# Two-layer spectral MLP on one core: background work kept out of a block's last two steps, activations and table work tied behind other instructions

## The chip, the cores and the metric

The kernel runs on one core of a Trainium2 chip. The metric is the device time of one launch in microseconds (us). Three runs of the kernel before gave 1007.89, 1008.41 and 1009.72 us, so the median is 1008.41 us. One more execution was recorded by the profiler; every row below is from that one.

## The reference, cut to what matters

```python
X = np.fft.fft(x, axis=1); X = np.fft.fft(X, axis=2)   # x: 2 x 3008 x 256
x = X.real.reshape(6016, 256)
h = x @ w_in;  x = np.maximum(h, 0.0) ** 2 @ w_out      # first layer, d_ff 2048
h = x @ w_in2; out = (h - np.tanh(h)) @ w_out2          # second layer, d_ff 2048
```

## The kernel before, in words

Every matrix product is made of three products of split numbers: an operand is held as a high part (an fp32r copy) and a low part (the operand minus that copy). Work on the 6016 positions goes in 8 blocks of twice 376 or 378 columns. The first 508 us of the trace hold the transform and the first layer, the rest the second layer.

The first layer is a list of 128 steps, `STEPS`: step i is a pair (block, f), f being one of 16 slices of the hidden dimension. The order is block 0 (f 0 to 3) in steps 0 to 3, block 1 in steps 4 to 19, the rest of block 0 in steps 20 to 31, and then blocks 2 to 7 with 16 steps each. So a block, or a part of block 0, ends in steps 3, 19, 31, 47, 63, 79, 95, 111 and 127. Steps 20, 48 and 80 begin with the transform of the next two blocks (lines L352 writing `a`), which keeps TensorE busy for 7 to 10 us.

Step i of the loop runs these parts:

- `front` of step i+2 on TensorE (L352, 6 matmuls into `w`);
- for the steps in `MADE` one slice of `w_in` is made: `transform_in` (L247) needs the bits that `conv` assembled on VectorE (L227, L229, L231);
- `mid` of step i+2: three sums on VectorE (L490, L491, L492, each with an operand in PSUM), then on ScalarE a Relu (L498) and two squares (L499 writes the high part `gh`, L500 the full square);
- `back` of step i on TensorE (L520): 8 matmuls with `gh` of step i and 4 with `gl` of step i-1, and in a block's last step 4 more with its own `gl`. The first step of a block needs the accumulators `a` free;
- after a block's last step `evac`: ScalarE copies two accumulators and VectorE the other two (L551) to `y`, and a DMA stores them;
- `late` of step i+1: the low part `gl` on GpSimd (L509, 1.925 us on average), in the first steps on VectorE.

Beside that runs background work that later stages need. It is cut into pieces by Python generators, and each step takes one or two pieces: `bg0` (rows of the transform's even half, `xf`, L319 to L328), `bg1` (the next batch, L302 to L328), `bg2` (L337), `bg3` (the second layer's weights: the bits in L227 to L231, the low parts in L578, sums of quarters in L586 to L595), and `x7_next` (the second layer's input of a block, L616 to L638). Nearly all of it runs on VectorE, with one operand copy on ScalarE (L219, L335, L576, L593, L623) that feeds it or waits for it.

The order on each engine is not the order of the program: a scheduler lists the instructions by its own estimate, and may put a later instruction in front. `tc.issue_after(ins)` is the one rein: the instructions traced in its block stand behind `ins` on the engine of `ins`. The loop already used it with the last sum of the step's `mid` (`last_mid`, on VectorE) for the pieces of `bg0` to `bg3`, except where a step needs all the rest at once (steps 20, 48 and 80), and not for `x7_next`.

Of the kernel before, what the change touches and what calls it, by code (L numbers as in the profile page):

```python
# [20 lines left out]
NF = DFF // 128  # L21
# [30 lines left out]
STEPS = [(0, f) for f in range(HALF)] + [(1, f) for f in range(NF)]  # L52
# [86 lines left out]
def spectral_mlps(  # L139
# [8 lines left out]
    pe, act, dve, pool, sp = nc.tensor, nc.scalar, nc.vector, nc.gpsimd, nc.sync  # L148
# [36 lines left out]
    def step(gen, k=1000):  # L185
        for _ in range(k):
            if next(gen, "end") == "end":
                return
# [13 lines left out]
    def wt_alloc(layer, f):  # L202
        wt[f] = main.tile([128, 4, 256], F32R, tag=f"wt{f}", name=f"wt{layer}_{f}")
# [246 lines left out]
    last_mid = [None]  # L450
# [60 lines left out]
    def ends(blk, f):  # L511
        return f == NF - 1 or blk == 0 and f in LAST
# [32 lines left out]
    def evac(blk, add=False):  # L545
        n = NC[BLOCKS[blk][1]]
        for m in range(2):
            y = main.tile([128, 2, NM], F32, tag="y", name="y", bufs=2)
            for s in range(2):
                a = acc[1, blk][m][s][:, :n]  # L550
                act.copy(y[:, s, :n], a) if m == 0 else dve.tensor_copy(y[:, s, :n], a)  # L551
            dst = x2_d[blk][:, m, :].rearrange("p (s n) -> p s n", s=2)
            if add:
                pool.dma_start(dst, y[:, :, :n], accum_op=ALU.add)
            else:
                sp.dma_start(dst, y[:, :, :n])

# [231 lines left out]
    n = NC[BLOCKS[0][1]]  # L791
# [10 lines left out]
    def even_rows():  # L802
        for t in range(3):
            yield from folds[t]
            yield from split_even(0, t)

    def next_batch():
        for t in range(3):
            load_x(1, t)
        for t in range(3):  # L810
            yield from fold(1, t)

    def next_even():
        for t in range(3):
            yield from split_even(1, t)

    bg0, bg1, bg2, bg3 = even_rows(), next_batch(), next_even(), make_w2()
# [5 lines left out]
    def look(i):  # L823
        if i < NS and i not in fronts:
            fronts.add(i)
            front(*STEPS[i])

    for i in range(-2, NS - 2):
        blk, f = STEPS[i] if i >= 0 else (0, i)
        if i == max(MADE) + 2:  # L830
            wstack.close()
            pools["w"] = wstack.enter_context(tc.tile_pool(name="psb", bufs=2, space=PSUM))
        look(i + 2)
        if i in MADE:
            p = wps[STEPS[i + 2]]
            w = MADE[i]
            wt_alloc(1, w)
            transform_in(w, p)
            split_transformed_hi(w, p)

        if (blk, f) in DFT:
            for b2 in DFT[blk, f]:
                if b2 == 4:
                    step(bg1)
                    for t in range(3):
                        dft_pair(4, t)
                    step(pair_evac(4))
                else:
                    step(bg0 if b2 < 4 else bg2)
                    dft_mm(b2)  # L850
                    dft_evac(b2)
            look(i + 3)
        mids = mid(*STEPS[i + 2])
        step(mids, 1)
        if i >= 0:
            back(blk, f)
        if i >= 0 and ends(blk, f):
            evac(blk, blk == 0 and f == NF - 1)
        step(mids)
        if i >= -1:  # L860
            late(*STEPS[i + 1])

        if i + 4 in MADE and i + 4 > 1:
            load_raw(1, MADE[i + 4])
        if i in MADE:
            split_transformed_lo(w, p)
            split_hi(w, 2, val[1, w][:, 256:])
        if i + 2 in MADE and i + 2 > -1:
            conv_abs(1, MADE[i + 2])
        if i in MADE:  # L870
            split_lo(w, 2, val[1, w][:, 256:])
            middle_load(w)
        if i == -2:
            middle_add(1)
        if i - 1 in MADE:
            middle_add(MADE[i - 1])
        if i + 1 in MADE and i + 1 > -2:
            step(conv(1, MADE[i + 1]))

        if i >= 8:  # L880
            with tc.issue_after(last_mid[0].ins):
                if i < NF + HALF:
                    step(bg0, 1)
                elif i < 3 * NF:
                    step(bg1, 2)
                else:
                    if blk == 3:
                        step(bg2, 1)
                    step(bg3, 2)
        if blk == NBLK - 1:  # L890
            if f > 0:
                restore(f - 1)
            if f >= 8:
                load_sums(f - 8)
            if f == 3:
                x7_next = make_x7(0)
            if f > 3:
                step(x7_next, 2)

        if i in TABS:  # L900
            for t in range(3):
                load_table(TABS[i], t)
# [21 lines left out]
    for blk in range(NBLK):  # L924
        for j in range(NF // 2):
            if blk < NBLK - 1 and j == 1:
                x7_next = make_x7(blk + 1)
# [31 lines left out]
```

## Time and profile before

| what | value |
|---|---|
| three runs | 1007.89, 1008.41, 1009.72 us |
| the profiled execution's own time | 1006.97 us |
| its span, first to last instruction | 1005.1 us |
| TensorE busy | 963.3 us (96%) |
| VectorE busy | 787.4 us (78%) |
| ScalarE busy | 726.7 us (72%) |
| GpSimd busy | 251.6 us (25%) |
| mean granted TensorE clock | 0.995 |

TensorE is busy nearly all the time, so what can be won is its idle time. It is read by stage, with the engine that each idle time waited for, and then in the timeline around that point.

### The profile page before, as it was taken

The page shows a single profiled execution, that of the slowest core. Times are in us where ns is not written, and L with a number is a line of the kernel's source. Part 1 is how long each engine was busy: PE and PEld are TensorE (multiplying, and loading weights), DVE is VectorE, ACT ScalarE, POOL GpSimd, SP SyncE. Part 2 cuts the span into 40 slices and gives each one's busy share as a digit, 9 for nine tenths or more (in the row PEclk, how much of TensorE's full clock was granted, in tenths as well). Part 3 has the DMA queues.
Part 4 walks back from the last instruction along what each step waited for, and adds up shares of the span by engine and source line. Part 5 has one row for each costly group of instructions (what it writes and reads, how often), then busy time and mean ns, then how long its engine had stood idle before and what let it go on. Part 6 is the DMA issues. An engine that isn't in the chain of part 4 may idle for free.

```text
span 1005.1 us, 15446 instructions
## 1 busy us (share of the span) xinstructions
PE 963.3 (96%) x5542; PEld 950.5 (95%) x5542; DVE 787.4 (78%) x1483; ACT 726.7 (72%) x1289; POOL 251.6 (25%) x171
## 2 busy tenths in 40 slices
PE   4998899899999999999999999999999999999998
PEld 3888898899999999999999999999999999999998
DVE  6999679757988688997576978769787797877766
ACT  2886767787888778897866767667676676766665
POOL 1144614653566546565500000000000000000000
PEclk9999999999999999999999999999999999999999
DMA  8674240205332422417620100001000010000000
GB/s 308 212 228 126 53 142 25 32 1 217 130 130 106 145 85 109 175 73 274 207 94 1 62 1 30 34 1 62 1 32 31 1 63 1 3 29 1 32 1 31
DMA packets 36332, 82.66 MB, mean 82 GB/s; under 512 B 7328, under 2 KB 21152, under 8 KB 36256
## 3 DMA queue, kind: packets, MB, share of 16 engines
q1 hardware_dynamic: 35280, 79.34, 22.5%
q0 software_dynamic: 976, 2.34, 1.4%
q8 instruction: 43, 0.70, 0.3%
q14 instruction: 33, 0.27, 0.1%
HBM read 55.97 MB, written 25.69 MB: 81 GB/s over the span
## 4 chain that ended last, share of the span: by engine, by line
PE 80%; DVE 12%; issue 3%; ACT 2%; DMA 2%; POOL 0%; SPq 0%; DVEq 0%; POOLq 0%; ACTq 0%
PE w L352 32%; PE a L352 29%; PE a L520 18%; DVE pb L490 2%; DVE h L491 2%; DVE h L492 1%; DMA p<-x 1%; DVE val L231 1%; DVE val L229 1%; DMA stage<-w 1%; ACT gh L499 1%; DVE p L321 1%; DVE wt L238 1%; PE w L247 1%; DMA mcol<-wt 0%
## 5 line engine op out<-in xcount | busy, mean ns | idle before, releaser
L509 POOL TENSOR_TENSOR gl<-h,gh 128x752 fp32r<-128x752 f32 (+1 forms) x120 | 230.0, 1925 | 195.2 <-ACT h L500 135.3
L352 PE MATMUL a<-gh,wt 128*128 128x376 f32 (+1 forms) x1024 | 259.7, 335 | 0.0
L520 PE MATMUL a<-gh,wt 128*128 128x376 f32 (+1 forms) x1024 | 204.4, 341 | 15.1 <-ACT gh L499 5.8
L520 PEld LDWEIGHTS a<-gh,wt 128*128 128x128 f32 x1024 | 179.4, 191 | 21.0 <-ACT gh L499 8.7
L352 PEld LDWEIGHTS a<-gh,wt 128*128 128x128 f32 x1024 | 184.7, 188 | 0.0
L352 PE MATMUL a<-gl,wt 128*128 128x376 f32 (+1 forms) x512 | 171.7, 335 | 0.0
L352 PE MATMUL w<-x,sums 128*128 128x376 f32 (+1 forms) x768 | 163.5, 334 | 0.0
L352 PE MATMUL w<-uv,wt 128*128 128x376 f32 (+1 forms) x777 | 157.1, 337 | 1.7 <-POOL wt L259 1.0
L498 ACT ACTIVATE h<-h 128x752 f32<-128x752 f32 (+1 forms) x125 | 103.8, 831 | 59.8 <-DVE h L492 59.1
L673 DVE TENSOR_TENSOR gl<-h,gh 128x376 fp32r<-128x376 f32 (+1 forms) x256 | 138.2, 545 | 11.2 <-ACT gh L671 10.6
L671 ACT CAST gh<-h 128x376 fp32r<-128x376 f32 (+1 forms) x256 | 129.3, 507 | 18.5 <-DVE h L669 17.6
L667 ACT ACTIVATE tanh<-h 128x376 f32<-128x376 f32 (+1 forms) x192 | 99.3, 519 | 56.6 <-DVE h L663 51.9
L352 PEld LDWEIGHTS w<-uv,wt 128*128 128x128 f32 x777 | 136.8, 190 | 2.8 <-POOL wt L259 1.3
L669 DVE TENSOR_TENSOR h<-h,tanh 128x376 f32<-128x376 f32 (+1 forms) x192 | 106.4, 555 | 40.0 <-ACT tanh L667 34.7
L352 PEld LDWEIGHTS w<-x,sums 128*128 128x128 f32 x768 | 135.5, 188 | 0.2 <-ACT u L701 0.2
L490 DVE SCALAR_TENSOR_TENSOR pb<-ub,w,w 128x376 f32<-128x376 f32 (+1 forms) x125 | 75.1, 601 | 56.5 <-PE w L352 48.6
L520 PE MATMUL a<-gl,wt 128*128 128x376 f32 (+1 forms) x512 | 109.1, 336 | 0.5 <-POOL gl L509 0.5
L500 ACT ACTIVATE h<-h 128x752 f32<-128x752 f32 (+1 forms) x128 | 106.8, 834 | 3.0
L499 ACT ACTIVATE gh<-h 128x752 fp32r<-128x752 f32 (+1 forms) x128 | 106.9, 835 | 2.9
L663 DVE TENSOR_TENSOR h<-u,w 128x376 f32<-128x376 f32 (+1 forms) x128 | 69.4, 542 | 38.8 <-ACT u L701 38.8
L352 PEld LDWEIGHTS a<-gl,wt 128*128 128x128 f32 x512 | 96.4, 188 | 0.4 <-DVE gl L673 0.3
L520 PEld LDWEIGHTS a<-gl,wt 128*128 128x128 f32 x512 | 90.8, 190 | 0.8 <-POOL gl L509 0.8
(98 smaller groups left out, 1082.6 us busy)
## 6 DMA issues: line engine op xcount, KB each, us to landing
stage<-w SPq DMA_DIRECT2D x32, 512.0 KB, 3.7
tab<-tab SPq DMA_DIRECT2D x12, 752.0 KB, 7.2
w2s<-w SPq DMA_DIRECT2D x16, 512.0 KB, 2.6
wt<-w2s SPq DMA_DIRECT2D x16, 512.0 KB, 3.6
sums<-sums SPq DMA_DIRECT2D x15, 512.0 KB, 3.8
tab<-tab SPq DMA_DIRECT2D x6, 756.0 KB, 5.4
x<-y SPq DMA_DIRECT2D x12, 376.0 KB, 3.6
x2f<-x SPq DMA_DIRECT2D x6, 752.0 KB, 4.7
```

The source lines that it names most:

```text
L352: pe.matmul(dst, a, r, start=(first and i == 0), stop=(last and i == 3 * len(terms) - 1), **kw)
L490: dve.scalar_tensor_tensor(pb[:, :n], ub[:, :n], w128[:, f:f + 1], bank(p, 0)[:, :n], ALU.mult, ALU.add)
L498: act.activation(h[:, :, :n], h[:, :, :n], AF.Relu)
L499: act.activation(gh[:, :, :n], h[:, :, :n], AF.Square)
L500: act.activation(h[:, :, :n], h[:, :, :n], AF.Square)
L509: eng.tensor_tensor(gl[:, :, :n], h[:, :, :n], f32(gh[:, :, :n]), ALU.subtract)
L520: pe.matmul(acc[1, blk][m][s][:, :n], wt[f][:, wi, m * 128:(m + 1) * 128], g[:, s, :n], start=first and k == 0, stop=last and k == len(par ...
L663: dve.tensor_tensor(h, c, d, ALU.add)
L667: act.activation(th, c, AF.Tanh)
L669: dve.tensor_tensor(h, c, th, ALU.subtract)
L671: act.copy(gh, h)
L673: dve.tensor_tensor(gl, h, f32(gh), ALU.subtract)
```

## The change

The change has four parts. Steps 8 to 17 take two pieces of `bg0` instead of one. No piece of `bg0` to `bg3` runs in a step that ends a block or in the step before (steps 18, 19, 30, 31, 46, 47, 62, 63, 78, 79, 94, 95, 110, 111). The activations of `mid` that are traced in a block's last step stand behind ScalarE's last copy of the accumulators. And the remaining pieces in steps 20 and 80, and those of `x7_next`, stand behind the step's sums.

```diff
@@ evac
-                act.copy(y[:, s, :n], a) if m == 0 else dve.tensor_copy(y[:, s, :n], a)
+                if m == 0:
+                    copied = act.copy(y[:, s, :n], a)
+                else:
+                    dve.tensor_copy(y[:, s, :n], a)
...
+        return copied
@@ the loop over steps
-                    step(bg0 if b2 < 4 else bg2)
+                    with tc.issue_after(last_mid[0].ins):
+                        step(bg0 if b2 < 4 else bg2)
...
-            evac(blk, blk == 0 and f == NF - 1)
+            copied = evac(blk, blk == 0 and f == NF - 1)
+            with tc.issue_after(copied.ins):
+                step(mids)
         step(mids)
...
-        if i >= 8:
+        if i >= 8 and not any(ends(*STEPS[k]) for k in (i, i + 1)):
             with tc.issue_after(last_mid[0].ins):
                 if i < NF + HALF:
-                    step(bg0, 1)
+                    step(bg0, 2)
...
             if f > 3:
-                step(x7_next, 2)
+                with tc.issue_after(last_mid[0].ins):
+                    step(x7_next, 2)
```

VectorE at the end of block 3 (steps 62 to 64), the kernel before. `w` are the sums' operands in PSUM, `w_2926` and `sums` the second layer's weights, `a_2451` and `a_2452` two accumulators.

```order
L578 TENSOR_TENSOR w_2926<-val,w_2926 128x2x256
L586 TENSOR_TENSOR sums<-val 128x128
L587 TENSOR_TENSOR sums<-val 128x128
L490 SCALAR_TENSOR_TENSOR pb<-ub,w_69,w_2964 128x376
L491 TENSOR_TENSOR h<-w_2965,pb 128x376
L492 TENSOR_TENSOR h<-pb,w_2965 128x376
L589 TENSOR_TENSOR sums<-sums,val 128x128
L591 TENSOR_TENSOR sums<-val,sums 128x128
L551 COPY y<-a_2451 128x376
L551 COPY y<-a_2452 128x376
L490 SCALAR_TENSOR_TENSOR pb<-ub,w_69,w_3011 128x376
```

The same place with the change. L554, L582, L590 and L591 are the lines L551, L578, L586 and L587 of before.

```order
L490 SCALAR_TENSOR_TENSOR pb<-ub,w_69,w_2959 128x376
L491 TENSOR_TENSOR h<-w_2960,pb 128x376
L492 TENSOR_TENSOR h<-pb,w_2960 128x376
L554 COPY y<-a_2451 128x376
L554 COPY y<-a_2452 128x376
L490 SCALAR_TENSOR_TENSOR pb<-ub,w_69,w_3002 128x376
L491 TENSOR_TENSOR h<-w_3003,pb 128x376
L492 TENSOR_TENSOR h<-pb,w_3003 128x376
L582 TENSOR_TENSOR w_2926<-val,w_2926 128x2x256
L590 TENSOR_TENSOR sums<-val 128x128
L591 TENSOR_TENSOR sums<-val 128x128
```

Five background instructions left the two steps ahead of the copies; the first three stand in the new block's first step now.

ScalarE at the same end, before: L219 and L593 are background work, the two L551 the copies.

```order
L498 ACTIVATE h<-h 128x2x376
L499 ACTIVATE gh<-h 128x2x376
L219 ACTIVATE val<-stage 128x512
L500 ACTIVATE h<-h 128x2x376
L498 ACTIVATE h<-h 128x2x376
L593 CAST sums<-sums 128x512
L551 COPY y<-a_2449 128x376
L551 COPY y<-a_2450 128x376
L499 ACTIVATE gh<-h 128x2x376
L500 ACTIVATE h<-h 128x2x376
```

And with the change, where L552 is the copy:

```order
L498 ACTIVATE h<-h 128x2x376
L499 ACTIVATE gh<-h 128x2x376
L500 ACTIVATE h<-h 128x2x376
L552 COPY y<-a_2449 128x376
L552 COPY y<-a_2450 128x376
L498 ACTIVATE h<-h 128x2x376
L499 ACTIVATE gh<-h 128x2x376
L500 ACTIVATE h<-h 128x2x376
```

A Relu and a cast that stood ahead of the copies stand behind them or later.

VectorE in steps 9 and 10, before. `xf_835` and its `p` are a fold of the transform, L227 to L231 assemble the bits of a slice of `w_in`.

```order
L490 SCALAR_TENSOR_TENSOR pb<-ub,w_69,w 128x376
L238 TENSOR_TENSOR wt_12_883<-val,wt_12_883 128x256
L491 TENSOR_TENSOR h<-w,pb 128x376
L492 TENSOR_TENSOR h<-pb,w 128x376
L321 TENSOR_TENSOR p<-p 128x256
L227 TENSOR_SCALAR cy<-stage 128x512
L229 SCALAR_TENSOR_TENSOR val<-val,cy 128x512
L231 SCALAR_TENSOR_TENSOR val<-stage,val 128x512
L490 SCALAR_TENSOR_TENSOR pb<-ub,w_69,w 128x376
```

The same stretch with the change:

```order
L492 TENSOR_TENSOR h<-pb,w 128x376
L323 TENSOR_TENSOR xf_835<-p 128x256
L324 TENSOR_TENSOR xf_835<-p 128x1
L326 TENSOR_TENSOR xf_835<-p 128x128
L327 TENSOR_TENSOR xf_835<-p 128x127
L328 TENSOR_TENSOR xf_835<-p 128x1
L238 TENSOR_TENSOR wt_12_888<-val,wt_12_888 128x256
L227 TENSOR_SCALAR cy<-stage 128x512
L229 SCALAR_TENSOR_TENSOR val<-val,cy 128x512
L490 SCALAR_TENSOR_TENSOR pb<-ub,w_69,w 128x376
L231 SCALAR_TENSOR_TENSOR val<-stage,val 128x512
```

Five instructions of the fold come one and two steps earlier, and L231, on which the next L247 of TensorE waits, moves behind the next step's first sum.

## Rows read from the trace of the kernel before

**Rows 1.** Stages: busy us of PE, PEld, DVE, ACT, POOL; clock, DMA share, GB/s.
```profile
56.00:126.00 70.00, 60.55 (x347) 58.37 (x347) 59.72 (x107) 50.12 (x75) 38.18 (x39) 0.95 0.44 125
...
454.00:508.00 54.00, 52.06 (x292) 51.61 (x292) 34.68 (x59) 42.58 (x57) 28.51 (x16) 0.97 0.67 232
508.00:1005.00 497.00, 493.58 (x2859) 492.87 (x2858) 381.72 (x763) 339.18 (x737) 0.00 (x0) 1.00 0.07 24
```
**Rows 2.** Who waited for whom: total us, times, longest us.
```profile
PE w L247 <- DVE val L231: 7.7, 5, 4.0
...
PE a L520 <- ACT gh L499: 5.8, 6, 1.5
...
PE a L520 <- ACT y L551: 5.0, 3, 2.9
...
PE a L520 <- DVE y L551: 4.2, 3, 2.0
```
**Rows 3.** TensorE's timeline: start, duration, line, count, idle before and its releaser.
```profile
178.48 1.68 PE L520 MATMUL a<-gh,wt 128*128 128x378 f32 x8 [2.88 <-ACT y L551]
...
291.05 1.67 PE L520 MATMUL a<-gh,wt 128*128 128x376 f32 x8 [1.75 <-ACT y L551]
...
452.61 1.18 PE L352 MATMUL w<-uv,wt 128*128 128x376 f32 x6
...
455.94 2.04 PE L520 MATMUL a<-gh,wt 128*128 128x376 f32 x7 [1.97 <-DVE y L551]
457.77 2.08 PE L352 MATMUL w<-uv,wt 128*128 128x376 f32 x6
```
**Rows 4.** VectorE's timeline at the end of block 6.
```profile
449.93 1.92 DVE L578 TENSOR_TENSOR w<-val,w 128x512 fp32r<-128x512 f32 x1
...
454.46 0.96 DVE L589 TENSOR_TENSOR sums<-sums,val 128x128 f32<-128x128 f32 x1
455.34 0.99 DVE L551 COPY y<-a 128x378 f32<-128x378 f32 x2
```
**Rows 5.** ScalarE's timeline at the end of block 0.
```profile
177.23 0.83 ACT L499 ACTIVATE gh<-h 128x756 fp32r<-128x756 f32 x1
177.97 0.83 ACT L551 COPY y<-a 128x376 f32<-128x376 f32 x2
```
**Rows 6.** Timeline of one VectorE line at two places, and of GpSimd beside the second.
```profile
148.14 0.43 DVE L323 TENSOR_TENSOR xf<-p 128x256 f32<-128x256 f32 x1
...
181.24 4.28 DVE L323 TENSOR_TENSOR xf<-p 128x256 f32<-128x256 f32 x1
...
180.63 4.59 POOL L509 TENSOR_TENSOR gl<-h,gh 128x756 fp32r<-128x756 f32 x2
```
**Rows 7.** Timeline of the start: first and last of seven fold instructions, then three waits.
```profile
22.57 0.42 DVE L319 TENSOR_TENSOR p<-p 128x256 f32<-128x256 f32 x1
...
35.96 0.15 DVE L328 TENSOR_TENSOR xf<-p 128x1 f32<-128x1 f32 x1
...
88.20 2.08 PE L247 MATMUL w<-val,wtab 128*128 128x128 f32 x8 [4.04 <-DVE val L231]
...
105.19 0.66 ACT L219 ACTIVATE val<-stage 128x512 f32<-128x512 f32 x1 [3.32 <-DMA stage<-w]
...
106.63 1.65 PE L520 MATMUL a<-gh,wt 128*128 128x376 f32 x8 [1.49 <-ACT gh L499]
```
**Rows 8.** Timeline of a step without a block's end: TensorE, and VectorE before it.
```profile
266.64 1.66 PE L520 MATMUL a<-gh,wt 128*128 128x376 f32 x8 [1.28 <-ACT gh L499]
...
259.43 1.91 DVE L586 TENSOR_TENSOR sums<-val 128x128 f32<-128x128 f32 x1
261.25 0.28 DVE L587 TENSOR_TENSOR sums<-val 128x128 f32<-128x128 f32 x1
```
**Rows 9.** VectorE's groups from 230 to 470 us: busy us, mean ns, idle before.
```profile
L231 DVE SCALAR_TENSOR_TENSOR val<-stage,val 128x512 int32<-128x512 int32 x16 | 15.3, 954 | 0.0
...
L625 DVE TENSOR_TENSOR x<-x2f,x 128x752 fp32r<-128x752 f32 x6 | 5.6, 933 | 0.0
```

## The prediction

> **What bounds the kernel now.** I read the busy time by stage first, then who waited for whom, then the timeline around each wait of TensorE. From 508 us on TensorE is busy for 493.58 of 497 us [rows 1]: the second layer has nothing to give, and all that can be won lies in the idle time of TensorE before that, 41.8 us over the span (1005.1 less 963.3) less those 3.4. Four waits matter [rows 2]. For the copies of the accumulators (`y`) it is 5.0 us behind ScalarE and 4.2 us behind VectorE, six waits at five block ends (the end of step 95 has two). For `gh` it is 5.8 us in six waits, and for the bits of `w_in` (L231) 7.7 us.
>
> Why the copies are late can be seen at two ends. At the end of block 6 VectorE runs a low part (L578) for 1.92 us and a sum (L589) for 0.96 us ahead of its two copies, which start at 455.34 [rows 4]; TensorE has finished its front at about 453.8 and idles 1.97 us [rows 3]. At the end of block 0 ScalarE runs a square of a later step before its copies, which start at 177.97 [rows 5], and TensorE idles 2.88 us [rows 3]. So background work on VectorE, and the activations that it delays, stand between the last matmul and the copies.
>
> A second row explains why such background work is dear. One and the same instruction, L323, takes 0.43 us at 148.14 and 4.28 us at 181.24; beside the second, GpSimd runs two low parts for 4.59 us from 180.63 on [rows 6]. VectorE's work with both operands in SBUF stands still while GpSimd works. Every piece of background work here is of that kind; the three sums, with an operand in PSUM, are not.
>
> **The change part by part.** Durations are from the profiled execution, 1006.97 us (1005.1 of span and 1.87 around it). It lies 1.44 us under the median of the runs, 1008.41; I take the difference that I work out from the median.
>
> *Block ends.* The two steps ahead of a copy hold no background work now, and ScalarE's copies stand ahead of the Relu. At stake are 5.0 + 4.2 = 9.2 us [rows 2]. What is late next is the copies themselves: two on VectorE take 0.99 us [rows 4], two on ScalarE 0.83 us [rows 5], and TensorE's front, which it runs meanwhile, takes 1.18 us [rows 3]. So the copies are just covered. I leave 0.2 us at each of five ends for their start and count a gain of 8.2 us; the ends are 9.2 and, if half the lateness comes from elsewhere, 4.6. The wait that the change adds holds the Relu, its squares and, behind them, GpSimd's low parts until the copies are done; they are wanted two steps later, which pays for 0.83 us of copies. At the ends of steps 19, 47 and 79 the transform of 7 to 10 us covers all of it as before.
>
> *The clock behind the last of these ends.* After the idle 1.97 us six matmuls take 2.08 us where 1.18 is usual [rows 3], and the granted clock of that stage is 0.97 [rows 1]: 0.03 x 54 = 1.6 us are lost at the lower of its levels. Without the idle time ahead of it I expect this to go in two cases of three: a gain of 1.1, between 0 and 1.6.
>
> *Start.* Seven fold instructions of 0.42 down to 0.15 us, about 2.0 us together, leave the stretch from 22.57 to 36 us [rows 7], where TensorE waits for VectorE. They come back in steps 9 to 15. There L231 of one slice of `w_in` stands behind five fold instructions and a sum, about 2.0 us, and TensorE already idles 4.04 us for it at 88.20 [rows 7]. The two cancel at that point: the wait stays near 4 us. Behind it something does improve. ScalarE waits 3.32 us for a load (L219, background) ahead of the first square of a step, and TensorE then idles 1.49 us for `gh` [rows 7]; in the new order this L219 stands behind both squares of that step, so one more step is fed before ScalarE stops. The load is also asked for later, so part of the wait stays. I count a gain of 1.5 us. The ends are a gain of 5.2 (2.0, 1.49 and half of the 0.05 x 70 = 3.5 us lost to the clock in this stage [rows 1]) and a loss of 2.0 (L231 late with nothing won before).
>
> *Pieces that move into the blocks.* `bg3` makes eight groups of sums (L586 to L595). Four stood at block ends (steps 62, 78, 94 and 110) and four inside blocks. Now all eight stand inside. One of the inner four costs a wait of 1.28 us, behind a sum that took 1.91 us where its neighbour took 0.28 [rows 8]; the other three share at most the rest of the 5.8 us [rows 2], less 1.49 and 1.28, that is 3.0 us, and the waits of the start are in that too. So one costs between 0.32 and 1.07 us on average. I take 0.4 and a loss of 1.6 us for the four that move, between 0 and 5.1 (four at 1.28).
>
> *The last block.* Eight steps skipped put `bg3`'s end at step 120 instead of 112, and the eight instructions of `x7` for block 0, which the scheduler had put as early as step 81, are tied to steps 117 to 122 now. Block 7 so receives 13 instructions of `bg3` and 8 of `x7`; three of `x7` for block 1 leave it. At 0.94 us each, the mean of their groups with what GpSimd holds up in it [rows 9], that is 18 x 0.94 = 16.9 us against 54.00 - 34.68 = 19.3 us in which VectorE idles [rows 1]. It fits as a whole but not locally: 13 of them stand in four steps, 12.2 us against 4 x 19.3/16 = 4.8. The overload of 7.4 us meets a look-ahead of two steps (2 x 54/16 = 6.8 us), part of which the sums and activations need. So the loss lies between 0 and 7.4; I take 1.2 us, the row nearest to it being the 1.28 us behind two burdened steps [rows 8]. SP's queue: the stores of the last weights and the reloads that follow them slip by the same eight steps, and are wanted a whole pair of slices (497/64 = 7.8 us) apart. No cost.
>
> *Work that moves into the second layer.* `x7` of block 1, eight instructions or 7.5 us, is no longer done ahead. VectorE has 497 - 381.72 = 115 us idle there, and GpSimd runs nothing [rows 1], so nothing is held up. It is wanted one block (497/8 = 62 us) later: no cost. Should that cover fail, each us on VectorE ahead of its sums would show on TensorE, 7.5 at most.
>
> Sum: -8.2 - 1.1 - 1.5 + 1.6 + 1.2 = -8.0 us, so 1008.4 - 8.0 = 1000.4 us.
>
> **The rivals.**
>
> *A: the stalls move instead of vanishing.* If GpSimd's low part meets each moved group, the four cost 5.1 instead of 1.6 and the last block half its overload, 3.7 instead of 1.2: 1000.4 + 3.5 + 2.5 = 1006.4 us. For it speaks that the same instruction took ten times as long beside GpSimd [rows 6], against it that three of four inner groups cost little. The Trainium skill says the same as a rule, in SBUF — State Buffer, section Who interferes with whom: a VectorE instruction with two SBUF inputs contends with a GpSimd instruction that reads SBUF, and issue order, not the shape of the instruction, decides who blocks. By that rule moving the work wins nothing unless it lands beside an idle GpSimd; the trace agrees that it blocks (4.28 us), and shows too that it need not meet (0.43 us).
>
> *B: all goes.* Ends 9.2, clock 1.6, start 5.2, nothing lost: 16.0 us, or 992.4 us. For it: the losses are two chance meetings. Against it: VectorE stays the limit around 88 us.
>
> *C: slower, by the last block.* The 21 instructions follow the sums in ten neighbouring steps. If six of these steps are held as long as the instruction of 4.28 us (3.85 over its 0.43 each, 23.1 us), the work is 40.0 us against 19.3 idle; less the look-ahead of 6.8 that is a stall of 13.9 instead of 1.2, and the time 1013.1 us. It decides from the sixth such hold on, since five give 10.1 and 1009.3 us. Against it: the held instructions at the other places took 1.9 us [rows 4, 8], and the long one met two low parts in a row [rows 6].
>
> *D: the change does not do what it says.* If the accumulators' wait merely changes its releaser, say to GpSimd's last low part, the first two terms go: 1008.4 - 1.5 + 2.8 = 1009.7 us.
>
> **How the numbers follow.** Forecast (995.5 to 1004) 0.62; A 0.13; B 0.15; C 0.05; D 0.05. A measurement tells 0.2%, or 2.0 us, from no change: faster is under 1006.4. The forecast, B and two thirds of A are faster: 0.62 + 0.15 + 0.09 = 0.86. The same are a third of A and D: 0.04 + 0.05 = 0.09. Slower is C, 0.05. The range from 993.5 to 1006.0 leaves out C, D, the upper third of A and a third of B, 0.19 together.
>
> **What would show it.** Right: the waits of TensorE for `y` fall from 9.2 to about 1 us, and around the block ends VectorE's copies directly follow the sums; the clock of the stage that holds the last block is 1.00; one wait of about 4 us for L231 remains near 88 us. Wrong: new waits for `gh` of 1 us and more one to three steps after a block's start (A), TensorE under 50 of 54 us busy in the last block (C), or waits for `y` that stay (D). If TensorE idles in the first 60 us of the second layer, the term of zero for `x7` was wrong.

## The result and the profile after

The changed kernel took 997.93 us (median of 6 runs, 997.11 to 1003.17), the kernel before, beside it, 1008.61 us (6 runs, 1006.5 to 1009.72): a ratio of 0.991, 95% interval 0.9888 to 0.9933. Forecast were 1000.4 us, between 993.5 and 1006.0. By the medians 10.7 us were gained where 8.0 were forecast. The profiled execution took 997.11 us, with a span of 995.3 (before 1005.1), so between the two traces it is 9.8 us.

In the changed file the lines behind `evac` have higher numbers: the copies are L552 (ScalarE) and L554 (VectorE), and L578, L586, L595, L625, L630 are L582, L590, L599, L629, L634.

Busy time by stage after, columns as in [rows 1]:

```profile
56.00:126.00 70.00, 60.28 (x359) 58.96 (x358) 62.55 (x115) 51.64 (x80) 39.20 (x39) 0.95 0.48 126
...
454.00:508.00 54.00, 49.56 (x279) 47.37 (x278) 45.72 (x73) 39.87 (x63) 21.16 (x12) 1.00 0.74 253
508.00:1005.00 497.00, 483.75 (x2804) 483.06 (x2802) 376.84 (x752) 333.01 (x724) 0.00 (x0) 1.00 0.06 21
```

The stage with the last block fell from 52.06 to 49.56 us of TensorE work although the kernel is faster. Its clock is 1.00 where it was 0.97. (In the third row the span ends at 995.3, so 487.3 us hold 483.75 of work: 3.55 idle, before 3.5.)

Who waited for whom, answering [rows 2]:

```profile
PE w L247 <- DVE val L231: 9.9, 5, 5.7
PE a L520 <- ACT gh L499: 5.9, 6, 2.1
...
PE w L352 <- DVE h L492: 1.7, 2, 1.1
PE a L520 <- ACT y L552: 0.9, 1, 0.9
```

The 9.2 us of waits for `y` are 0.9 (one wait, 0.93 at 172.87). The waits for `val` grew from 7.7 to 9.9; those for `gh` are as long as before, but lie elsewhere, as TensorE's timeline shows:

```profile
87.27 2.07 PE L247 MATMUL w<-val,wtab 128*128 128x128 f32 x8 [5.72 <-DVE val L231]
...
109.28 0.95 PE L520 MATMUL a<-gh,wt 128*128 128x376 f32 x4 [2.05 <-ACT gh L499]
...
259.94 1.64 PE L520 MATMUL a<-gh,wt 128*128 128x376 f32 x8 [1.21 <-ACT gh L499]
...
471.61 1.63 PE L520 MATMUL a<-gh,wt 128*128 128x376 f32 x8 [1.01 <-ACT gh L499]
...
480.44 1.65 PE L520 MATMUL a<-gh,wt 128*128 128x376 f32 x8 [1.00 <-ACT gh L499]
...
497.74 0.78 PE L352 MATMUL w<-x,sums 128*128 128x376 f32 x3 [0.51 <-ACT u L705]
```

Two of the five new waits of the last block stand here (the others, for VectorE's sums, are 0.21, 0.59 and 1.11); together they are 3.92 us. What a good block end looks like is seen at the end of block 6, where now the copies wait for TensorE and not TensorE for them (ScalarE, then VectorE):

```profile
440.56 0.85 ACT L552 COPY y<-a 128x378 f32<-128x378 f32 x2 [1.02 <-PE a L520]
...
440.73 1.01 DVE L554 COPY y<-a 128x378 f32<-128x378 f32 x2 [1.18 <-PE a L520]
```

The last block is crowded. VectorE's, GpSimd's and ScalarE's rows there (start, duration, idle time before and what ended it):

```profile
462.84 1.90 DVE L590 TENSOR_TENSOR sums<-val 128x128 f32<-128x128 f32 x1
465.12 2.35 POOL L509 TENSOR_TENSOR gl<-h,gh 128x752 fp32r<-128x752 f32 x1 [0.53 <-ACT h L500]
465.72 2.16 DVE L634 TENSOR_TENSOR x2f<-x2f 128x376 f32<-128x376 f32 x1
...
468.89 0.82 ACT L627 CAST x<-x2f 128x752 fp32r<-128x752 f32 x1 [3.90 <-DVE x2f L635]
469.24 0.53 DVE L492 TENSOR_TENSOR h<-pb,w 128x376 f32<-128x376 f32 x1
469.86 0.83 ACT L498 ACTIVATE h<-h 128x752 f32<-128x752 f32 x1 [0.15 <-DVE h L492]
...
472.94 2.03 POOL L509 TENSOR_TENSOR gl<-h,gh 128x752 fp32r<-128x752 f32 x1 [5.47 <-ACT h L500]
473.19 2.18 DVE L638 TENSOR_TENSOR x2f<-x2f 128x376 f32<-128x376 f32 x1
...
477.72 0.82 ACT L627 CAST x<-x2f 128x752 fp32r<-128x752 f32 x1 [2.38 <-DVE x2f L640]
478.69 0.83 ACT L498 ACTIVATE h<-h 128x752 f32<-128x752 f32 x1 [0.15 <-DVE h L492]
```

L634, L638 and L640 take 0.54 us alone and 1.9 to 2.2 beside a low part on GpSimd, L590 takes 0.28 alone and 1.90 here. They stand ahead of a step's sums in VectorE's queue. The Relu (L498) waits for the last sum, the high part for the Relu, and TensorE for the sum and the high part. ScalarE idles 3.90 and 2.38 us in front of its cast of `x7` (L627), but the cast is not what makes the Relu late: it ends at 469.71, the last sum only at 469.77, and both times the Relu waits another 0.15 us for that sum. What is late is VectorE.

### The profile page after: what moved, and what is told of

Same layout as the page of the kernel before. It is cut to its first block, busy times and chain, and to the rows that moved or that the text cites. A ratio compares the mean times of both kernels' runs of the same rounds, so it can differ in the third digit from the quotient of the medians.

```text
span 995.3 us, 15440 instructions
## 1 busy us (share of the span) xinstructions
PE 958.9 (96%) x5542; PEld 947.2 (95%) x5542; DVE 787.3 (79%) x1483; ACT 724.6 (73%) x1289; POOL 250.2 (25%) x171
## 4 chain that ended last, share of the span: by engine, by line
PE 82%; DVE 10%; ACT 3%; DMA 2%; issue 2%; SPq 0%; POOL 0%; DVEq 0%; ACTq 0%; POOLq 0%
PE w L352 33%; PE a L352 30%; PE a L520 20%; DVE pb L490 1%; DVE h L491 1%; DVE h L492 1%; ACT gh L499 1%; DMA p<-x 1%; DVE val L229 1%; DMA x2f<-x 1%; PE w L247 1%; ACT h L498 1%; DVE val L231 0%; DVE wt L238 0%; DVE xf L326 0%
## 5 line engine op out<-in xcount | busy, mean ns | idle before, releaser
L352 PE MATMUL a<-gh,wt 128*128 128x376 f32 (+1 forms) x1024 | 259.7, 335 | 0.0
L352 PEld LDWEIGHTS a<-gh,wt 128*128 128x128 f32 x1024 | 184.4, 188 | 0.3 <-ACT gh L675 0.3
L352 PE MATMUL a<-gl,wt 128*128 128x376 f32 (+1 forms) x512 | 171.4, 335 | 0.0
L352 PE MATMUL w<-x,sums 128*128 128x376 f32 (+1 forms) x768 | 163.6, 334 | 0.5 <-ACT u L705 0.5
L352 PE MATMUL w<-uv,wt 128*128 128x376 f32 (+1 forms) x777 | 156.4, 335 | 2.5 <-DVE h L492 1.7
L677 DVE TENSOR_TENSOR gl<-h,gh 128x376 fp32r<-128x376 f32 (+1 forms) x256 | 138.3, 545 | 10.7 <-ACT gh L675 10.0
L352 PEld LDWEIGHTS w<-uv,wt 128*128 128x128 f32 x777 | 135.6, 188 | 4.3 <-DVE h L492 2.3
L352 PEld LDWEIGHTS w<-x,sums 128*128 128x128 f32 x768 | 135.4, 188 | 0.8 <-ACT u L705 0.8
L498 ACT ACTIVATE h<-h 128x752 f32<-128x752 f32 (+1 forms) x125 | 103.6, 829 | 39.1 <-DVE h L492 36.3
L352 PEld LDWEIGHTS a<-gl,wt 128*128 128x128 f32 x512 | 96.5, 188 | 0.4 <-DVE gl L677 0.3
```

The lines of the kernel that those rows point to most:

```text
L352: pe.matmul(dst, a, r, start=(first and i == 0), stop=(last and i == 3 * len(terms) - 1), **kw)
L498: act.activation(h[:, :, :n], h[:, :, :n], AF.Relu)
L677: dve.tensor_tensor(gl, h, f32(gh), ALU.subtract)
```

## The experiments

All but one were timed in five rounds against the kernel before, whose median was 1008.8, 1008.38, 1008.44 and 1006.5 us in the four jobs. "Start" is the time from the first full group of the first product to the first transform of the second field (lines L352 writing `a`, 13.37 to 123.51 us in the kernel after) in the one profiled execution.

| run | median us | ratio, interval | waits for y | start |
|---|---|---|---|---|
| before | 1008.61 | | 9.2 | 112.56 |
| after | 997.93 | 0.991 (0.9888 to 0.9933) | 0.9 | 110.14 |
| e1 guard | 1004.31 | 0.9959 (0.9942 to 0.9977) | 7.5 | 112.07 |
| e2 pin | 1011.12 | 1.0022 (1.0001 to 1.0042) | 9.1 | 113.55 |
| e8 guard and pin | 1002.26 | 0.994 (0.9923 to 0.9957) | 6.3 | 110.68 |
| e3 start | 1005.68 | 0.9973 (0.9955 to 0.9991) | 8.7 | 110.68 |
| e4 after, x7 free | 1001.02 | 0.9932 (0.9913 to 0.995) | 5.5 | 111.30 |
| e5 early list | 996.49 | 0.9883 (0.9866 to 0.99) | 0.9 | 110.38 |
| e6 late list | 999.19 | 0.9909 (0.9892 to 0.9925) | 0.9 | 111.03 |
| e7 e5 and e6 | 997.67 | 0.989 (0.9869 to 0.9911) | 0.9 | 110.88 |
| e10 gl on VectorE | 1001.57 | 0.9929 (0.9905 to 0.9952) | 0.9 | 112.43 |
| e11 e5 and e10 | 998.78 | 0.9902 (0.9881 to 0.9923) | 0.9 | 111.42 |
| e12 e5 and a late L219 | 995.66 | 0.9881 (0.9858 to 0.9903) | 0.9 | 109.33 |

### The block ends: which edit frees the copies

**e1**, only the steps without background work (from step 20 on):

```diff
-        if i >= 8:
+        if i >= 8 and not (i >= 20 and any(ends(*STEPS[k]) for k in (i, i + 1))):
```

> The kernel before with the guard alone, from step 20 on (no background piece in a block's last two steps; start, copies and x7 as before). Theory T, VectorE's background work is what delays the copies: TensorE's waits for y fall from 9.2 us to between 1.5 and 4 us (the first end keeps its 0.5, and x7 pieces that nothing ties still stand at the ends of blocks 5 and 6), the last block has no wait over 0.5 us, and the time falls by 5 to 8 us. Rival R, the place of ScalarE's copies is what counts: 4 us or more of the 5.0 us behind ScalarE's y stay, and the time falls by 2 to 4 us.

Measured 1004.31 us, 4.5 less than before, between what theory T and rival R have. By the waits it is rival R: they fall to 7.5 us only, not to 4. VectorE's waits for its copies are gone but for one of 0.5, and ScalarE's took their place (7.0 us in three waits), since the Relu and the squares of a later step still stand ahead of its copies:

```profile
177.85 1.67 PE L520 MATMUL a<-gh,wt 128*128 128x378 f32 x8 [2.62 <-ACT y L551]
...
453.07 3.26 PE L520 MATMUL a<-gh,wt 128*128 128x376 f32 x8 [2.29 <-ACT y L551]
```

**e2**, only the activations behind ScalarE's copies:

```diff
-            evac(blk, blk == 0 and f == NF - 1)
+            copied = evac(blk, blk == 0 and f == NF - 1)
+            with tc.issue_after(copied.ins):
+                step(mids)
```

> The kernel before with the activations tied behind ScalarE's copies alone. T: the waits for y stay at 7 us or more of 9.2, since VectorE's background work still stands ahead of its copies and delays ScalarE's inputs; the time moves by less than 1.5 us. R: the waits behind ScalarE's y fall from 5.0 to under 1.5 us and the time falls by 3 to 5 us.

Measured 1011.12 us, no gain (2.3 us more, the interval just above 1), and waits of 9.1 us, as theory T has it. Now VectorE's copies are late behind background work (4.4 us, and 1.2 at a transform where there was none), and ScalarE's still cost 3.5:

```profile
291.79 1.69 PE L520 MATMUL a<-gh,wt 128*128 128x376 f32 x8 [1.92 <-ACT y L552]
...
406.63 1.59 PE L520 MATMUL a<-gh,wt 128*128 128x378 f32 x7 [1.74 <-DVE y L554]
```

**e8**, both together, nothing else changed.

> The kernel before, with the two edits at the ends of blocks together and nothing else (no background work in a block's last two steps from step 20 on; the activations behind ScalarE's copies); the start and x7's place as before. Each of these alone gave 1004.3 and 1011.1 against 1008.8. Theory T (each edit alone leaves the other engine late: without background work ScalarE's copies still stand behind activations, with the copies first VectorE's still stand behind background work, so that the gain is in the two together): y waits of 9.2 us fall to some 3 or 4 (x7's pieces still stand ahead of VectorE's copies at the ends of blocks 5 and 6, as in the changed kernel without x7's tie), no waits in the last block, 1002 to 1004. Rival R (the parts add): 1004.3 and +2.3 us make 1006 to 1007.

Measured 1002.26 us: theory T's range, under the rival's 1006. The waits for `y`, 6.3 us, stayed above its 3 or 4. Alone the two give 0.9959 x 1.0022 = 0.9981, together 0.994: about 4 us (give or take 3) come only when both are there: TensorE's wait ends with whichever engine's copies are last. Still late are the ends of blocks 5 and 6, where pieces of `x7` stand ahead of VectorE's copies and its casts ahead of ScalarE's.

**e4**, the changed kernel with the pieces of `x7` free again:

```diff
             if f > 3:
-                with tc.issue_after(last_mid[0].ins):
-                    step(x7_next, 2)
+                step(x7_next, 2)
```

> The changed kernel with x7 not tied. T, the last block's new waits (3.9 us) come from x7 and bg3 meeting in four steps: they fall under 0.5 us, the ends of blocks 5 and 6 get 1 to 2 us of waits for y back because x7 pieces land there again, and the time is 994 to 997 us against 997.9. Rival, bg3's shift alone makes them: 3 us of the last block's waits stay and the time is 998 to 1000 us.

Measured 1001.02 us, 3.1 more than the changed kernel. The same two ends are late as in e8, and the last block has no wait at all (TensorE 54.00 of 54 us busy):

```profile
396.06 2.55 PE L520 MATMUL a<-gh,wt 128*128 128x378 f32 x8 [2.10 <-ACT y L552]
...
449.27 0.44 PE L520 MATMUL a<-gh,wt 128*128 128x376 f32 x1 [1.32 <-ACT y L552]
...
450.95 2.40 PE L520 MATMUL a<-gh,wt 128*128 128x376 f32 x7 [1.24 <-DVE y L554]
```

So the tie of `x7` moves a stall from two block ends (4.66 us) into the last block (3.92 us, and 0.51 behind it). The waits alone are nearly the same. What differs between the two traces is the clock behind them: matmuls of 2.55 and 2.40 us that take some 1.6 at the full clock, 0.97 in the 113 us from 341 to 454, which is 3.4 us, against 1.00 in the changed kernel. e8, with the same two stalls, has 0.97 there too; whether the place of the stall decides it or the execution is not shown. I had expected that the kernel without the tie would be the faster one; it isn't.

### The last block: can its loss be avoided

**e5**, the changed kernel with `bg3` begun 12 steps earlier:

```diff
-                elif i < 3 * NF:
+                elif i < 3 * NF - 12:
                     step(bg1, 2)
```

> The changed kernel, with the pieces of the fourth background list (bg3, the table work of the last part of the first layer) begun at step 36 instead of step 48, two a step as before, so that they end some 12 steps earlier and the last block has only the pieces of x7 behind its products. Theory T (the 3.9 us of waits that the change brings into the last block come from two kinds of background work in the same steps: VectorE's operations wait beside GpSimd's, ScalarE's cast waits for them, and the copies of gh stand behind the cast): TensorE's five waits between 468 and 481 fall to at most 1 us together, and the time to 993 to 996. Rival R (the casts of x7 alone hold ScalarE: 3.90 and 2.38 us of its waits stand behind x7's own two sums on VectorE): three of the five waits stay, 2.5 us or more, and the time is 996.5 to 999. If the pieces only bring the same stalls to earlier steps (rival A of the prediction), new waits for gh of over 1 us stand between steps 36 and 48, and the time doesn't change.

Measured 996.49 us, at the rival's edge by time, theory T by the waits in the trace: the five are gone, two of 0.27 and 0.38 us stand at 484 and 488. But 1.20 us come back at the first product of the second layer, and the waits for `gh` between 257 and 266 are 2.50 us where they were 1.21. The first of these:

```profile
491.51 1.30 PE L352 MATMUL w<-x,sums 128*128 128x376 f32 x6 [1.20 <-ACT m L686]
```

Of the 4.4 us that the kernel after loses in the last block and at the second layer's beginning, 2.4 are left there, 0.58 of them in another wait at 495, and about one more stands near 260. The intervals of e5 and of the changed kernel overlap, so that e5 is the faster one is likely, not shown.

### The hold: VectorE beside GpSimd

**e9**, a GpSimd operation added in one block of the second layer, where GpSimd otherwise rests (a single run):

```diff
             act.copy(gh, h)
+            if blk == 2:
+                s = main.tile([128, 512], F32, tag="xf2", name="probe")
+                pool.tensor_tensor(s[:, :n], f32(gh), f32(gh), ALU.subtract)
```

> The changed kernel with one operation added for each product of the second layer's third block (32 of them): GpSimd subtracts gh from itself into a scratch tile that nobody reads. The other blocks of the second layer have no GpSimd work, and are the control. There the subtraction with both inputs in SBUF (h<-h,tanh) has a mean of 548 ns, gl<-h,gh one of 545, and those with one input in PSUM (h<-w,tanh and h<-u,w) 548 and 542. Theory T (a VectorE operation that reads two SBUF tiles is held while a GpSimd operation runs, one with an input in PSUM is not): in the third block the first two have means of 800 ns or more, with single ones of 1.2 us or more, the other two stay at 540 to 560; TensorE waits there and the kernel is 3 to 12 us longer. Rival R (the long operations of the first layer come from the DMA traffic or the tiles of that stage, not from GpSimd): all four stay at 540 to 560.

VectorE's groups from 622 to 690 us (busy us, mean ns, idle before), where the 32 added operations lie:

```profile
L680 DVE TENSOR_TENSOR gl<-h,gh 128x378 fp32r<-128x378 f32 x32 | 22.5, 705 | 1.4 <-ACT gh L675 1.1
L673 DVE TENSOR_TENSOR h<-h,tanh 128x378 f32<-128x378 f32 x24 | 14.3, 602 | 3.6 <-ACT tanh L671 3.5
L667 DVE TENSOR_TENSOR h<-u,w 128x378 f32<-128x378 f32 x16 | 8.7, 542 | 2.8 <-ACT u L708 2.8
L673 DVE TENSOR_TENSOR h<-w,tanh 128x378 f32<-128x378 f32 x8 | 4.4, 550 | 2.4 <-ACT tanh L671 2.3
```

The operations with both inputs in SBUF went from 547 and 550 ns (these shapes in the kernel after) to 705 and 602, single ones to 1.16 us; those with an input in PSUM stayed at 542 and 550. The direction is theory T's, the size smaller than its 800, probably because the added operations are short (0.8 to 1.2 us) and many VectorE operations miss them. The run took 1005.71 us; in its trace the second layer is 3.4 us longer than in the changed kernel's (506.8 against 503.4), the rest lies ahead of the added work. The Trainium skill (SBUF — State Buffer, section Who interferes with whom) states both halves: a VectorE operation with two SBUF inputs contends with a GpSimd operation that reads SBUF, one with at most one, outside VectorE's two-port modes, does not. This run agrees: 705 against 547, 550 against 551 ns.

One row lies outside this pair: L227, which reads a single SBUF tile and takes 0.42 us alone, took 1.88 at 454.96 in the kernel after, beside a low part of 1.81 at 454.74. So the prediction's sentence that every piece of background work has both operands in SBUF does not hold, and such a piece can be held too; why was not tried.

### The start: what bounds it

**e3**, only the edits of the start (two pieces of `bg0` a step, none in steps 18 and 19, the rest in step 20 behind the sums).

> The kernel before with the change of the start alone (two pieces of bg0 in steps 8 to 17, none in steps 18 and 19, the rest in step 20 tied). T: the transform of step 20 begins 2 to 3 us earlier than in a profile of before (126.8), the wait for L231 near 88 us is 5 to 6 us instead of 4.04, a second half-clock stretch is missing, and the time falls by 1.5 to 2.5 us. Rival: the gain of the start seen after the change is the luck of where the clock's lower stretch falls; the time moves by less than 1 us.

Measured 1005.68 us, 0.9973. The interval, 0.9955 to 0.9991, stays below 1. In the trace the start is 1.9 us shorter than before (110.68 against 112.56), but e8, with the old start, has 110.68 too: one trace doesn't give the size. At the end of block 6 the wait of 1.97 us for `y` is there as before, but the matmuls behind it ran at the full clock (stage 1.00 where it was 0.97). Behind two other waits, as long as before, it fell where it had not. One of them:

```profile
176.24 2.66 PE L520 MATMUL a<-gh,wt 128*128 128x378 f32 x8 [2.88 <-ACT y L551]
```

Before, these eight took 1.68 us [rows 3]; at 401.03 seven took 2.14 where it was 1.58; the stages from 126 to 230 and from 341 to 454 have 0.98 here where they had 1.00. So the stretches at the lower clock moved, and in this trace they cost more than before, not less.

**e6**, the changed kernel with `bg0` in steps 13 to 17, four pieces each, and **e7**, that and e5:

```diff
                 if i < NF + HALF:
-                    step(bg0, 2)
+                    step(bg0, 4 if i >= 13 else 0)
```

> The changed kernel, with the first background list (bg0) asked for in steps 13 to 17, four pieces a step, instead of steps 8 to 17, two a step. Theory T (TensorE's wait of 5.72 us for val near 87 comes from background operations on VectorE that are held beside GpSimd's, 2.78 and 2.00 us where the same line takes 0.28 alone, ahead of the last operation of val): with no background work there the wait falls to 2 to 3 us and the start up to the first transform of the second field is 2 to 3 us shorter, 995 to 996; the pieces packed into five steps cost at most 1 us in waits for gh near 105 to 112. Rival R (val is late by its own chain and its load, the background work only lies in the idle time): the wait stays at 5 us or more, and the time at 997 to 999, or above it by what the packed pieces cost.

> The two edits of the runs before together: the fourth list begun at step 36, the first list packed into steps 13 to 17. If both terms are independent, the time is the changed kernel's less both gains: 990 to 993 by theory T, 996 to 999 by both rivals.

Measured 999.19 and 997.67 us. The wait of 5.72 us near 87 fell to 2.83, as theory T has it, and both times are in the rivals' ranges or above. The rows of e6:

```profile
80.72 4.69 DVE L231 SCALAR_TENSOR_TENSOR val<-stage,val 128x512 int32<-128x512 int32 x1
80.80 2.15 POOL L509 TENSOR_TENSOR gl<-h,gh 128x752 fp32r<-128x752 f32 x1
...
82.98 1.86 POOL L509 TENSOR_TENSOR gl<-h,gh 128x752 fp32r<-128x752 f32 x1
...
85.46 1.85 PE L247 MATMUL w<-val,wtab 128*128 128x128 f32 x8 [2.83 <-DVE val L231]
```

With no background work there, the hold falls on the operation of `val` itself: 4.69 us for an operation that takes 0.68, through two low parts of GpSimd. Counted from the first full group, this L247 begins 2.4 us earlier than in the kernel after (71.49 against 73.90), and what follows gives it back: ScalarE's wait for a load, 3.60 us at 98.59, came forward with the queue, TensorE waits 1.59 us for `gh` at 100.91 and 2.10 at 108.46, and the clock from 111 to 117 is 0.83 where it was 1.00. So by the trace rival R's reading, that the background work only lies in the idle time, is wrong at 87 us, and what it costs up to the transform stays open.

**e10**, the changed kernel with the low parts of steps 7 to 10 on VectorE, and **e11**, that and e5:

```diff
-        eng = dve if blk == 0 and f < NF // 2 else pool
+        eng = dve if blk == 0 and f < NF // 2 or STEPS.index((blk, f)) in (7, 8, 9, 10) else pool
```

> The changed kernel with the low halves gl of the four steps 7 to 10 computed on VectorE (0.94 us each) instead of GpSimd (1.8 to 2.1 us each), so that GpSimd has no long work around 75 to 85, and nothing else. Theory T (VectorE's held operations there, 1.52, 2.78, 2.00 and 1.24 us against 0.41, 0.28, 0.28 and 0.68 alone, some 5.9 us together, make val late): the held ones go, four times 0.94 us come, TensorE's wait of 5.72 us near 87 falls to 2 to 4 us; the first transform of the second field starts 1 to 3 us earlier, 995 to 997. Rival R (VectorE's queue is simply full there, whoever does the work): the wait stays at 5 us or grows, 998 or more.

> The edit of the run before together with the fourth list begun at step 36 (996.5 by itself). If the terms are independent the gain of the run before comes on top: 993.5 to 995.5 by theory T; 996.5 or more by rival R.

Measured 1001.57 and 998.78 us, both above theory T's ranges. The hold is gone where it was (L326 and L327 take 0.30 and 0.28 us now; they took 2.78 and 2.00 us in the kernel after, beside low parts at 79.85 and 82.16) and now falls on all three operations of `val`:

```profile
84.68 1.27 DVE L227 TENSOR_SCALAR cy<-stage 128x512 int32<-128x512 int32 x1
85.98 1.66 DVE L229 SCALAR_TENSOR_TENSOR val<-val,cy 128x512 int32<-128x512 int32 x1
...
87.38 1.89 POOL L509 TENSOR_TENSOR gl<-h,gh 128x752 fp32r<-128x752 f32 x1 [0.28 <-POOL xe L337]
87.68 2.14 DVE L231 SCALAR_TENSOR_TENSOR val<-stage,val 128x512 int32<-128x512 int32 x1
...
89.88 1.16 PE L247 MATMUL w<-val,wtab 128*128 128x128 f32 x8 [2.85 <-DVE val L231]
```

Alone they take 0.42, 0.69 and 0.68 us. The wait is 2.85 us, within theory T's 2 to 4, but L247 begins later than in the kernel after (75.39 against 73.90 from the first full group), and the start is 112.43: the four low parts cost VectorE 3.8 us, a wait of 1.03 for `wt` is new, and the wait for `gh` is 2.99 us at 109.95. That last one, 1.2 to 3.0 us near 110, stands in every kernel with the new start so far but e6 and e7, which have 2.10 and 0.58 near 108. Its rows in the kernel after:

```profile
106.97 0.67 ACT L219 ACTIVATE val<-stage 128x512 f32<-128x512 f32 x1 [2.74 <-DMA stage<-w]
107.55 0.81 ACT L498 ACTIVATE h<-h 128x752 f32<-128x752 f32 x1
```

This L219 is the first operation of `bg3` on ScalarE, traced for step 48. It is tied behind a VectorE instruction, which reins in VectorE alone, so the scheduler puts it here, ahead of a Relu, and its load (issued at 101.91) lands only at 106.97.

**e12**, e5 with this one operation behind the squares of the next step:

```diff
         for f in range(NF):
-            conv_abs(2, f)
+            if f == 0:
+                with tc.issue_after(held[0].ins):
+                    conv_abs(2, f)
+            else:
+                conv_abs(2, f)
...
+        if i == 15:
+            held.append(last_sq[0])
```

> The changed kernel with the fourth list begun at step 36 (996.5 by itself), and one edit more: the first operation of that list on ScalarE (L219, the absolute value of the second layer's first slice of weights), which the scheduler had put ahead of the activations of a step near 107, stands behind the squares of the step after, four activations later. Theory T (in every kernel so far ScalarE waits 1.9 to 3.8 us for the load that this L219 reads, and TensorE then 1.2 to 2.9 us for the gh of the activations behind it, whatever VectorE does before): that wait of TensorE, 1.27 us at 110.31 in the run with step 36, falls under 0.4 us, the first transform of the second field starts 0.8 to 2 us earlier counted from the first product, and the time is 994.5 to 995.8. Rival R (the start has one limit, VectorE's chain up to val, and the wait for gh only takes what that leaves): the waits move to another place between 95 and 125, the first transform starts as late as before, and the time is 996 to 997.

Measured 995.66 us. L219 runs at 114.13 and waits for nothing, the wait for `gh` near 110 is gone (the next, for `h`, is 0.27), and the start is 109.33 us, the shortest of all and 1.05 under e5:

```profile
102.83 1.16 PE L247 MATMUL w<-val,wtab 128*128 128x128 f32 x8 [1.11 <-DVE val L231]
...
109.62 1.27 PE L352 MATMUL w<-uv,wt 128*128 128x376 f32 x6 [0.27 <-DVE h L492]
```

Every number is in theory T's range, with 0.7 us of the 1.27 given back at 102.83 (0.39 in e5). That the wait near 110 came from this L219 is shown, since with it the wait went. That the start is shorter by it is not: half of the 1.05 us lies ahead of the wait near 87 (L247 begins at 74.04 and 74.58 from the first full group), where the edit changes nothing, and two executions of one program differ by more (110.14 and 112.78, the kernel after and e9). The ratio, 0.9881, can't tell it from e5 (0.9883). e5 and e12 have the lowest ratios of all, and e12's upper bound, 0.9903, is under the changed kernel's 0.991 but within its interval.

## Why the prediction was right, and where it was not

**Block ends** (8.2 forecast): 9.2 less 0.93 is 8.3. The size held, and e1, e2, e8 and e4 show that it takes three edits, which the prediction did not say: VectorE's guard alone leaves 7.5 of the 9.2 us, the pin alone 9.1, both 6.3. The tie of `x7`, which the prediction counted only as a load on the last block, frees the ends of blocks 5 and 6: without it 5.5 us stay (e4), with it 0.9. The tie alone was not run.

**The clock behind the last end** (1.1): the 0.97 of that stage is 1.00, 1.6 us, the upper bound. That is luck as much as the change: in e3, with the same wait of 1.97 us ahead of them, the matmuls ran at the full clock there, and e9, the changed kernel up to the second layer, has 0.97 in this stage again.

**Start** (1.5): 2.4 us by the two traces, and most of it is the clock. The stretch from 111 to 117 us was at 0.72 before and is at 1.00 after (0.28 x 6 = 1.7 us); e9, the same program up to there, has 0.72 again. Four profiled executions with the old start take 112.2 us on average (before, e1, e2, e8: 110.7 to 113.6), five with the new one 111.1 (after, e3, e4, e5, e9: 110.1 to 112.8): 1.2, less than either group spreads. So e3's time shows that the start gains something; its size is not settled. Rows of the kernel before:

```profile
78.36 2.25 DVE L319 TENSOR_TENSOR p<-p 128x256 f32<-128x256 f32 x1
...
82.31 2.60 DVE L321 TENSOR_TENSOR p<-p 128x256 f32<-128x256 f32 x1
...
86.01 2.14 DVE L231 SCALAR_TENSOR_TENSOR val<-stage,val 128x512 int32<-128x512 int32 x1
...
111.00:117.00 6.00, 5.69 (x25) 5.47 (x24) 4.74 (x8) 5.18 (x7) 4.19 (x4) 0.72 0.00 0
```

Of the reasoning, "the two cancel" held to the tenth of a microsecond: counted from the first full group, the product that waits for L231 begins at 73.94 us before and at 73.90 after. "The wait stays near 4 us" did not, and it doesn't follow: TensorE comes 1.7 us earlier (the L247 at 65.89 before, 63.27 after) to a point that stays where it was, so the wait grows by as much, from 4.04 to 5.72. Operations held beside GpSimd were there in both kernels: L319, L321 and L231 for 2.25, 2.60 and 2.14 us before, L321, L326, L327 and L231 for 1.52, 2.78, 2.00 and 1.24 after. The other half held: L219 now stands behind both squares of the step, and two waits for `gh` (1.49 and 1.52) became one of 2.05.

**Pieces that move into the blocks** (a loss of 1.6): nothing. Outside the start and the last block the waits for `gh` are 1.21 and 0.43 us (before 0.91, 1.28 and 0.38), and from 341 to 454 TensorE is busy throughout (113.00 of 113). The mean of four rows was no price for the next four: whether a piece meets a low part is decided case by case.

**The last block** (a loss of 1.2, at most 7.4): this is the term that was mis-sized; it measured 3.9. The working had the right engine and the local overload (7.4 us), then took the nearest row, 1.28, for a stretch of four overloaded steps with no such row. Four operations there (L590, L634, L638, L640) took 6.2 us more than alone, ahead of the sums. Half the overload, which stood under rival A, would have been nearer. e4 (no `x7` in these steps) and e5 (no `bg3` there) both lose the waits, so it is the two together that overload VectorE.

**The second layer** (0): right, 0.51 us at its beginning.

By the points that both traces share, the 9.8 us are 2.4 in the start (0.5 of the waits for `y` is in it, at 57.01 before), 7.1 from the first transform of the second field to the second layer's first product, less 0.6 behind that, and 0.9 before the first full product group (14.26 and 13.37), where nothing was changed. So the mechanism that carries the gain, the block ends, is the one forecast. That the total came so near is in part luck: the loss of 1.6 that did not come makes up for more than half of the 2.7 that the last block lost beyond its term, and the clock and those 0.9 us lie with the execution.

**The rivals.** A's mechanism is real, but only in the last block and at the start. B did not come. C named the right place, but six long holds were needed and there were four of some 2 us; its sign, TensorE under 50 of 54 us busy, did appear (49.56), and was badly chosen, because a stall of 3.9 us gives it as well as one of 13.9. D is out: `y` waits fell to 0.9.

## What to carry to other kernels

When several engines must all release one resource, an edit to one of them can show little (here 4.5 us for one, nothing for the other, 10.7 with all four parts): look at who is second, and change both before judging either. A moved piece of work costs what it costs in its new neighbourhood, so price it with the engine that it will run beside. When an engine idles ahead of an operation, look at what released the next one behind it before blaming the first: here ScalarE's long wait for a cast cost nothing, because the Relu behind it waited for VectorE anyway. And a tie to an instruction of one engine holds back only that engine: operations of the same list on other engines may run far ahead, and wait there for a load.

## What the hardware showed that was not expected

One program's first layer can differ by 4.3 us between two executions. e9 is the changed kernel up to the second layer, and from the first product group to the second layer's first product it took 482.9 us (14.28 to 497.14) where the profiled execution of the changed kernel took 478.5 (13.37 to 491.90). A part of that is the granted clock. Two stretches of the kernel after, then of e9 (last three columns: clock, DMA share, GB/s):

```profile
111.00:117.00 6.00, 6.00 (x37) 6.00 (x36) 3.61 (x7) 5.84 (x8) 5.59 (x4) 1.00 0.00 0
...
482.00:492.00 10.00, 10.00 (x60) 10.00 (x59) 4.87 (x10) 9.56 (x14) 7.25 (x5) 1.00 0.73 244
```

```profile
111.00:117.00 6.00, 5.75 (x24) 5.75 (x25) 2.15 (x7) 5.77 (x9) 4.81 (x3) 0.72 0.00 0
...
482.00:492.00 10.00, 8.63 (x40) 8.32 (x41) 6.22 (x12) 9.11 (x12) 5.44 (x3) 0.83 0.59 222
```

Both fall to the lower level (1.2 GHz) behind the idle time near 87 (0.59 and 0.57 from 84 to 92). e9 falls again behind its wait for `gh` at 111.25 (2.63 us idle ahead of it), and behind the waits of the last block at 484, and the kernel after does not, with idle times of 2.05 and 1.00 us there: 0.28 x 6 + 0.17 x 10 = 3.4 us. So the waits of two executions agree to some tenths of a microsecond, and the clock behind them need not. The times go with it: the eleven runs of the kernel before that stood beside e1 took 1004.8 to 1007.3 us at a mean granted clock of 0.995, and 1011.0 at 0.988. A difference of 1 or 2 us between two traces can be that alone.

A held VectorE operation can outlast one GpSimd operation: the 4.69 us of L231 in e6 end 0.6 us after the second of two low parts in a row. What decides whether it gets its turn between the two was not tried.
